# Attention and channel mix on one core: the receptance unit ahead of the tail scores, and two units in three pairs

## The chip, the cores and the metric

The kernel runs on one core of a Trainium2 chip. The metric is the device time of one execution in microseconds. The kernel before took 929.22 us, the median of three executions (929.09 to 930.02). One further execution was recorded by the hardware profiler; every duration below comes from it.

## The reference

Two layers follow each other, all in 32-bit floating point, with 8 sequences of 448 positions.

```python
# attention: 12 heads of 64, no softmax, a sigmoid instead
scores = scale * np.matmul(q, k.transpose(0, 1, 3, 2)) - np.log(S)
attn = 1.0 / (1.0 + np.exp(-scores))
x = np.matmul(attn, v)                    # heads side by side: [8, 448, 768]
# channel mix
xk = mu_k * x + (1.0 - mu_k) * x_prev     # x_prev: x one position earlier
xr = mu_r * x + (1.0 - mu_r) * x_prev
k = np.maximum(xk @ w_k, 0.0)             # 768 -> 1024
v = k * k @ w_v                           # 1024 -> 768
r = 1.0 / (1.0 + np.exp(-(xr @ w_r)))     # receptance, 768 -> 768
return r * v
```

The three weight matrices arrive as 64-bit floats, so the kernel turns their bits into 32-bit numbers itself.

## The kernel before

The two heads that share 128 partitions form a pair; there are 48 pairs, six to a sequence. Every 32-bit matrix product of the scores and of the channel mix is made from three products of a rounded high part and a low remainder (`hi`, `lo`), so each operand is prepared as two tiles: ScalarE rounds, VectorE subtracts (`prepare`, L295 and L296, for the queries and keys).

For pair n the attention loop puts onto TensorE, in this order: three chunks of scores for 128 keys each (`scores`, L322, six matmuls, both heads at once), the weighing of pair n-1 by its values (`weigh`, L351), in every even pair the tails of two pairs' weighing (`weigh_tails`, L360), the scores of the last 64 keys (`score_tail`, L331, three matmuls), and from pair 7 on one unit of the receptance (`receptance`, L386 to L388, 18 matmuls). A unit is one block of 128 output rows for one sequence; 40 units run in pairs 7 to 46, and the rest behind the loop. After two pairs' tails `gather` copies the sums out, mixes each position with its predecessor and splits the result into the units' operands `xr` (L369 to L375), kept for two sequences.

The scores live in three tiles of PSUM, `sc`, each with two halves of 512 columns. `turn(n, c)` picks the tile: chunks 0 to 2 and the tail (c = 3) of the pairs follow each other round the three. A chunk fills both halves, the tail only half 0, and the pair's unit uses half 1 of the tail's tile. ScalarE turns scores into weights (`sigmoid`, L343: `pf` for chunks, `pt` for the tail) and the unit's sums into `ro` (L392), which SyncE's queue stores to `r_d`.

The weights are converted during the loop, mostly on VectorE: first the 12 half rows of w_r (`convert_wr`, L222 to L226, L243 and L244), and then w_k and w_v (`convert_seven`), whose combinations go back to memory and are loaded again near the end of the loop and behind it.

All of this is handed to a small planner, `Plan`. Each operation has an engine, an estimated cost, a priority (mostly the pair number plus a fraction), and the keys that it reads and writes. The planner simulates the engines: whenever one is free, the ready operation of lowest priority starts. The simulated starts give the order in which the instructions are written out, and each engine runs its own in that order. Every TensorE operation of the loop also writes one key, "order", so these stay in the order in which the program names them. The waits on the chip are put in by the tile framework from the order of reads and writes of each tile.

Priorities of the w_r conversions go up by `WR_PACE`, those of the others by `W_PACE` per step. The second half of the kernel, from about 518 us on, is a stretch of matrix products with seven combinations per block (L592).

Of the kernel before, what the change touches and what calls it, by code (L numbers as in the profile page):

```python
# [10 lines left out]
AF = mybir.ActivationFunctionType  # L11
# [11 lines left out]
class Plan:  # L23
# [7 lines left out]
    def op(self, engine, cost, prio, run, reads, writes, dma=None):  # L31
        i = len(self.ops)
        deps = set()
        for r in reads:
            if r in self.writer:
                deps.add(self.writer[r])
        for w in writes:
            if w in self.writer:
                deps.add(self.writer[w])
            deps.update(self.readers.get(w, ()))  # L40
        for r in reads:
            self.readers.setdefault(r, []).append(i)
        for w in writes:
            self.writer[w] = i
            self.readers[w] = []
        deps.discard(i)
        self.ops.append(Op(engine, cost, prio, run, deps, dma))
# [50 lines left out]
def attention_then_channel_mix(  # L98
# [14 lines left out]
    nc = tc.nc  # L113
    P = 128
    N, _, S = q.shape
# [3 lines left out]
    NP = DM // P  # L119
# [4 lines left out]
    NC = S // P  # L124
# [21 lines left out]
    r_d = [[dram.tile([P, S], F32, name=f"r_d{i}_{b}") for b in range(B)] for i in range(NJ)]  # L146
# [3 lines left out]


    WP, PFB, PTB, LEAD = 512, 6, 4, 2
    WR_PACE, W_PACE = 0.45, 0.75
    LATE = 2


    def ring(pool, name, bufs, shape, dtype):
        return [pool.tile(shape, dtype, name=f"{name}{i}") for i in range(bufs)]
# [17 lines left out]
    ro = ring(rpool, "ro", 2, [P, S], F32)  # L176
# [5 lines left out]
    vn = ring(apool, "vn", 5, [P, NV, D], F32)  # L182
# [4 lines left out]
    pf = ring(apool, "pf", PFB, [P, 2, S], F32)  # L187
# [3 lines left out]
    sc = ring(pscore, "sc", 3, [P, 2, 512], F32)  # L191
    av = ring(psum, "av", 2, [P, 512], F32)

    plan = Plan()
    op = plan.op
    SP, PE, ACT, DVE = "SP", "PE", "ACT", "DVE"
    SWITCH = 190

    def mm(n, cols=S):
        return n * (cols * 0.447 + 3)  # L200

    def act(n, sbuf=False, ptr=False):
        return 51 + 0.834 * n + 42 * sbuf + 93 * ptr

    def dve(n, fast=False, ptr=False):
        return 69 + n / (1.92 if fast else 0.96) + 61 * ptr

    def dma(dst, src, prio, reads, writes):
        ns = dst.shape[0] * math.prod(dst.shape[1:]) * 4 / 300
        op(SP, 500, prio, lambda: nc.sync.dma_start(dst, src), reads, writes, dma=ns)  # L210
# [76 lines left out]
    def load(n, at):  # L287
        dma(kn[n % 2], k[n], at, [], [("kn", n % 2)])
        dma(qn[n % 2], q[n], at, [], [("qn", n % 2)])
        dma(vn[n % 5], v[n], at, [], [("vn", n % 5)])  # L290
# [9 lines left out]
    def pe(cost, go, reads, writes, at):  # L300

        op(PE, cost, at, go, reads, writes + ["order"])

    def products(n):
        i = n % LEAD
        return ((kh[i], qh[i]), (kl[i], qh[i]), (kh[i], ql[i]))

    def qk(n):
        i = n % LEAD
        return [(a, i) for a in ("kh", "kl", "qh", "ql")]  # L310


    def turn(n, c):
        return (n * (NC + 1) + c) % 3
# [11 lines left out]
    def score_tail(n, at):  # L326
        u = turn(n, NC)

        def go():
            for e, (kk, qq) in enumerate(products(n)):  # L330
                nc.tensor.matmul(sc[u][:, 0, :S], kk[:, NC * P:], qq, start=e == 0, stop=e == 2)  # L331

        pe(mm(3) + SWITCH, go, qk(n), [("sc", u, 0)], at)

    def sigmoid(n, c, at):
        u = turn(n, c)
        if c < NC:
            i = (n * NC + c) % PFB
            f, s, w, K, R = pf[i], sc[u][:, :, :S], 2 * S, ("pf", i), [("sc", u, 0), ("sc", u, 1)]
        else:  # L340
            i = n % PTB
            f, s, w, K, R = pt[i], sc[u][:, 0, :S], S, ("pt", i), [("sc", u, 0)]
        op(ACT, act(w), at, lambda: nc.scalar.activation(f, s, AF.Sigmoid, bias=NEG_LOG_S, scale=SCALE), R, [K])  # L343


    def weigh(n, c, at):
        i = (n * NC + c) % PFB

        def go():
            for h in range(2):  # L350
                nc.tensor.matmul(av[n % 2][half[h], :S], vn[n % 5][:, h * NC + c, :], pf[i][:, h, :], start=c == 0, stop=False)  # L351

        pe(900 + SWITCH * (c == 0), go, [("pf", i), ("vn", n % 5)], [("av", n % 2)], at)


    def weigh_tails(n, at):
        def go():
            for m in (n, n + 1):
                for r in range(2):
                    nc.tensor.matmul(av[m % 2][half[r ^ (m % 2)], :S], vn[m % 5][half[r], 2 * NC, :], pt[m % PTB][half[r], :], start=False, stop=True)  # L360

        reads = [x for m in (n, n + 1) for x in (("pt", m % PTB), ("vn", m % 5))]
        pe(950, go, reads, [("av", 0), ("av", 1)], at)

    def gather(n, at):
        b, j = divmod(n, NP)
        x, y = xx[n % 2], t1[n % 2]
        X, T = ("xx", n % 2), ("t1", n % 2)
        op(ACT, act(S), at, lambda: nc.scalar.copy(x[:, 1:], av[n % 2][:, :S]), [("av", n % 2)], [X])  # L369
        dma(x_d[j][b], x[:, 1:], at, [X], [("x_d", n)])  # L370
        op(ACT, act(S, True, True), at, lambda: nc.scalar.mul(y, x[:, :S], omr[:, j:j + 1]), [X, ("om", 0)], [T])  # L371
        op(DVE, dve(S, ptr=True), at, lambda: nc.vector.scalar_tensor_tensor(y, x[:, 1:], mur[:, j:j + 1], y, ALU.mult, ALU.add), [X, T], [T])  # L372
        t, key = xr[j][:, :, b % 2 * S:(b % 2 + 1) * S], ("xr", j, b % 2)
        op(ACT, act(S, True), at, lambda: nc.scalar.copy(t[:, 0], y), [T], [key + ("hi",)])
        op(DVE, dve(S), at, lambda: nc.vector.tensor_sub(t[:, 1], y, t[:, 0]), [T, key + ("hi",)], [key + ("lo",)])  # L375

    def receptance(b, i, at, bank):
        t, tk = bank
        u = (b * NJ + i) % 2
        rows = slice(i * P, (i + 1) * P)  # L380
        for j in range(NJ):
            keys = [("xr", j, b % 2, a) for a in ("hi", "lo")]

            def go(j=j):
                hi, lo = (xr[j][:, a, b % 2 * S:(b % 2 + 1) * S] for a in range(2))
                nc.tensor.matmul(t[:, :S], wr_hi[j][:, rows], hi, start=(j == 0), stop=False)  # L386
                nc.tensor.matmul(t[:, :S], wr_lo[j][:, rows], hi, start=False, stop=False)  # L387
                nc.tensor.matmul(t[:, :S], wr_hi[j][:, rows], lo, start=False, stop=(j == NJ - 1))  # L388

            nh = i * P // HN  # L390
            pe(mm(3), go, keys + [("wr", j, nh), (("wr", j, nh), "lo")], [tk], at)
        op(ACT, act(S), at, lambda: nc.scalar.activation(ro[u], t[:, :S], AF.Sigmoid), [tk], [("ro", u)])  # L392
        dma(r_d[i][b], ro[u], at, [("ro", u)], [("r_d", i, b)])

    ORDER = (0, 1, 5, 4, 6, 2, 3)
    POS = {p: g for g, p in enumerate(ORDER)}
# [24 lines left out]
    jt = 0.0  # L421
    for nh in range(2):
        for j in range(NJ):
            convert_wr(j, nh, jt)
            jt += WR_PACE
    jt = max(6, jt)
    for w, out7, half_rows, n in ((w_k, wk_o, NJH, DF // 2), (w_v, wv_o, NFH, HN)):
        for t in range(half_rows):
            convert_seven(w, out7, t, half_rows, n, W_PACE, jt + 0.4)
# [1 line left out]
    units = [(b, i) for b in range(B - 1) for i in range(NJ)]  # L431
    late = units[len(units) - LATE:]
    units = units[:len(units) - LATE]
    for n in range(N + 1):
        if n + 2 < N:
            load(n + 2, n + 0.2)
        if n < N:
            if n + 1 < N:
                prepare(n + 1, n + 0.6)
            for c in range(NC):  # L440
                scores(n, c, n)
                sigmoid(n, c, n + 0.1 * c)
        if n:
            for c in range(NC):
                weigh(n - 1, c, n)
            if n % 2 == 0:
                weigh_tails(n - 2, n)
                gather(n - 2, n + 0.45)
                gather(n - 1, n + 0.5)
        if n < N:  # L450
            score_tail(n, n)
            sigmoid(n, NC, n + 0.5)
        if n > NP and units:
            b, i = units.pop(0)
            u = turn(n, NC)
            receptance(b, i, n + 0.4, (sc[u][:, 1], ("sc", u, 1)))
    late = units + late
    for g in range(2):
        load_weight(0, ORDER[g], N - 6 + 3 * g)
# [87 lines left out]
    op = plan.op  # L547
    units = late + [(B - 1, i) for i in range(NJ)]
    banks = [(sc[i][:, h], ("sc", i, h)) for i in range(3) for h in range(2)]
# [4 lines left out]
        if g < AHEAD:  # L554
            right(0, 0, ORDER[g], 10 * g + 5)
    for u, (b, i) in enumerate(units):
        receptance(b, i, 10 * u, banks[u % 6])
    with tc.manual_schedule():
        plan.emit()
    psc.close()  # L560
# [16 lines left out]
    op = plan.op  # L577
# [67 lines left out]
    for stage in range(2):  # L645
        rows = DF // 2 // P if stage == 0 else HN // P
        for s in range(NS):
            for g, p in enumerate(ORDER):
                at = (stage * NS + s) * 7 + g
# [58 lines left out]
```

## Time and profile before

| | |
|---|---|
| median of three executions | 929.22 us |
| the profiled execution's own time | 932.01 us |
| its span | 930.2 us |
| mean granted TensorE clock | 0.990 |
| TensorE busy | 879.8 us |
| VectorE busy | 572.9 us |
| ScalarE busy | 500.4 us |

The span runs from the first to the last instruction of the execution. Busy time counts an engine's instructions; an engine's idle time before an instruction is put down to whatever released it last. Rows of a timeline give the start, the duration, the engine, the line, the operation with the tile that it writes and the tiles that it reads, and in brackets the idle time before it and who ended it. Rows of merged instructions have a count at the end. Rows of windows give the stretch, its length, the busy time (and instructions) of TensorE, its weight loads, VectorE, ScalarE and GpSimd, the granted clock, the share of the DMA engines and GB/s.

### The profile page before, as it was taken

The numbers are of one execution on the slowest core, as the hardware profiler recorded it, in microseconds if no ns is written. First come the engines' busy times: TensorE is split into PE (matmuls) and PEld (weight loads), VectorE is DVE, ScalarE is ACT, GpSimd is POOL, SyncE is SP. The second block draws the span as 40 slices with busy tenths as digits, with TensorE's granted clock in tenths as the row PEclk, the third lists the DMA queues.
The fourth block names the chain that finished last, engine by engine and source line by source line (L and its number), as shares of the span: only waits on it lengthen the run. The fifth ranks groups of instructions, "written<-read, shape, count | busy, mean of one in ns | idle before, by whom it ended". The sixth has DMA issues, their size and how long they took to land.

```text
span 930.2 us, 13102 instructions
## 1 busy us (share of the span) xinstructions
PE 879.8 (95%) x4656; PEld 684.6 (74%) x4656; DVE 572.9 (62%) x1039; ACT 500.4 (54%) x858; POOL 0.5 (0%) x8
## 2 busy tenths in 40 slices
PE   6889999999999999999989999999999999999998
PEld 3446566656665666566558899999999999999997
DVE  5999877852222232222225789696968978695955
ACT  5785666655565666556555756556464533233330
POOL 0000000000000000000000000000000000000000
PEclk8899999999999999999999999999999999999999
DMA  7679997863333434334127556334365556465514
GB/s 257 205 252 335 302 318 241 280 215 102 122 115 103 135 111 132 102 106 130 50 92 245 175 174 197 119 139 129 125 228 161 199 163 216 132 196 178 159 60 148
DMA packets 90929, 159.21 MB, mean 171 GB/s; under 512 B 10352, under 2 KB 73328, under 8 KB 90864
## 3 DMA queue, kind: packets, MB, share of 16 engines
q1 hardware_dynamic: 90864, 158.38, 52.6%
q8 instruction: 36, 0.59, 0.3%
q14 instruction: 29, 0.24, 0.1%
HBM read 99.62 MB, written 58.72 MB: 170 GB/s over the span
## 4 chain that ended last, share of the span: by engine, by line
PE 91%; ACT 4%; DVE 2%; issue 2%; DMA 1%; SPq 0%; POOLq 0%; POOL 0%; ACTq 0%; DVEq 0%
PE xb L592 25%; PE yb L592 19%; PE av L351 12%; PE sc L322 10%; PE sc L386 7%; PE sc L388 6%; PE sc L387 6%; PE sc L331 4%; ACT pt L343 2%; PE av L360 2%; DMA wraw<-in_moe_w_r 1%; DVE wbits L226 0%; SPq L210 0%; ACT t L371 0%; ACT pf L343 0%
## 5 line engine op out<-in xcount | busy, mean ns | idle before, releaser
L386 PE MATMUL sc<-xr,slot 128*128 128x448 f32 x288 | 110.7, 384 | 30.9 <-ACT pt L343 25.3
L517 ACT CAST rr<-ys 128x448 fp32r<-128x448 f32 x135 | 73.9, 567 | 105.0 <-PE yb L592 40.6
L343 ACT ACTIVATE pf<-sc 128x896 f32<-128x896 f32 x144 | 122.7, 920 | 12.7 <-PE sc L322 12.7
L351 PE MATMUL av<-pf,vn 128*64 128x448 f32 x576 | 121.4, 557 | 0.0
L372 DVE SCALAR_TENSOR_TENSOR t<-xx,mur,t 128x448 f32<-128x448 f32 x48 | 30.7, 681 | 136.7 <-ACT t L371 136.7
L387 PE MATMUL sc<-xr,slot 128*128 128x448 f32 x288 | 105.9, 368 | 0.0
L388 PE MATMUL sc<-xr,slot 128*128 128x448 f32 x288 | 105.8, 367 | 0.0
L592 PE MATMUL xb<-rr,slotb 128*128 128x448 f32 x450 | 93.4, 365 | 0.7 <-issue 0.7
L592 PE MATMUL yb<-rr,slot 128*128 128x448 f32 x450 | 93.9, 364 | 0.0
L296 DVE TENSOR_TENSOR kl<-kn,kh 128x512 fp32r<-128x512 f32 x48 | 33.1, 690 | 97.2 <-ACT kh L295 97.2
L386 PEld LDWEIGHTS sc<-xr,slot 128*128 128x128 f32 x288 | 54.4, 189 | 51.8 <-ACT pt L343 40.2
L518 DVE TENSOR_TENSOR rr<-ys,rr 128x448 fp32r<-128x448 f32 x135 | 80.4, 618 | 19.5 <-ACT rr L517 19.4
L592 PEld LDWEIGHTS xb<-rr,slotb 128*128 128x128 f32 x450 | 84.4, 188 | 7.7 <-issue 1.1
L592 PEld LDWEIGHTS yb<-rr,slot 128*128 128x128 f32 x450 | 84.4, 187 | 6.7
L351 PEld LDWEIGHTS av<-pf,vn 128*64 128x64 f32 x576 | 37.8, 139 | 61.5 <-issue 60.4
L322 PE MATMUL sc<-qh,kh 64*128 64x448 f32 x288 | 59.6, 410 | 7.5 <-ACT qh L295 6.6
L392 ACT ACTIVATE ro<-sc 128x448 f32<-128x448 f32 x48 | 26.2, 545 | 67.4 <-PE sc L388 59.9
L322 PE MATMUL sc<-ql,kh 64*128 64x448 f32 x288 | 55.1, 379 | 6.0 <-DVE ql L296 6.0
L343 ACT ACTIVATE pt<-sc 128x448 f32<-128x448 f32 x48 | 26.1, 545 | 60.7 <-PE sc L388 55.7
L388 PEld LDWEIGHTS sc<-xr,slot 128*128 128x128 f32 x288 | 54.5, 189 | 4.6
L387 PEld LDWEIGHTS sc<-xr,slot 128*128 128x128 f32 x288 | 54.6, 190 | 3.6
L322 PE MATMUL sc<-qh,kl 64*128 64x448 f32 x288 | 54.1, 372 | 1.1 <-DVE kl L296 1.1
(88 smaller groups left out, 1410.0 us busy)
## 6 DMA issues: line engine op xcount, KB each, us to landing
k_d<-cc SPq DMA_DIRECT2D x64, 224.0 KB, 2.0
kn<-in_k SPq DMA_DIRECT2D x48, 256.0 KB, 2.7
qn<-in_q SPq DMA_DIRECT2D x48, 224.0 KB, 3.2
vn<-in_v SPq DMA_DIRECT2D x48, 224.0 KB, 3.1
x_d<-xx SPq DMA_DIRECT2D x48, 224.0 KB, 3.2
r_d<-ro SPq DMA_DIRECT2D x48, 224.0 KB, 2.6
x<-x_d SPq DMA_DIRECT2D x48, 224.0 KB, 2.6
rt<-r_d SPq DMA_DIRECT2D x48, 224.0 KB, 2.9
```

What stands on the lines that cost most here:

```text
L296: op(DVE, dve(w), at, lambda src=src, hi=hi, lo=lo: nc.vector.tensor_sub(lo[i], src[n % 2], hi[i]), [(a + "n", n % 2), (a + "h", i)], [(a ...
L322: nc.tensor.matmul(sc[u][:, h, :S], kk[half[h], c * P:(c + 1) * P], qq[half[h], :], start=e == 0, stop=e == 2)
L331: nc.tensor.matmul(sc[u][:, 0, :S], kk[:, NC * P:], qq, start=e == 0, stop=e == 2)
L343: op(ACT, act(w), at, lambda: nc.scalar.activation(f, s, AF.Sigmoid, bias=NEG_LOG_S, scale=SCALE), R, [K])
L351: nc.tensor.matmul(av[n % 2][half[h], :S], vn[n % 5][:, h * NC + c, :], pf[i][:, h, :], start=c == 0, stop=False)
L372: op(DVE, dve(S, ptr=True), at, lambda: nc.vector.scalar_tensor_tensor(y, x[:, 1:], mur[:, j:j + 1], y, ALU.mult, ALU.add), [X, T], [T])
L386: nc.tensor.matmul(t[:, :S], wr_hi[j][:, rows], hi, start=(j == 0), stop=False)
L387: nc.tensor.matmul(t[:, :S], wr_lo[j][:, rows], hi, start=False, stop=False)
L388: nc.tensor.matmul(t[:, :S], wr_hi[j][:, rows], lo, start=False, stop=(j == NJ - 1))
L517: op(ACT, act(S, True), at, lambda: nc.scalar.copy(r[:, 0], y), [Y], [R])
L518: op(DVE, dve(S), at, lambda: nc.vector.tensor_sub(r[:, 1], y, r[:, 0]), [Y, R], [R + ("lo",)])
L592: nc.tensor.matmul(bank[:, :S], a, b, start=first and t == 0 and e == 0, stop=t == n - 1 and e == 2, skip_group_check=True)
```

## The change

In a pair with a unit, the unit's matmuls are now named before the tail's scores. Its sigmoid `ro` and its store are taken out of the function and called after the tail; `ro` also reads a new key, "tail", that the tail's scores write. Units start at pair 10 instead of 7: pairs 10 to 12 have two each, the first in half 1 of the tile of the next pair's first chunk, and pairs 13 to 46 one each, as before. The conversions of w_r get priorities 0.85 apart (0.45 before), those of w_k and w_v begin at 10.2 instead of 6 and stand 0.9 apart (0.75 before). Four cost estimates of the planner change: a weighing and the tails' weighing cost 752 (900 and 950 before), and the extra 190 for a change of the matmuls' shape goes from the tail's scores to a unit's first step.

```diff
-    WR_PACE, W_PACE = 0.45, 0.75
+    WR_PACE, W_PACE = 0.85, 0.9
+    R_FROM = 10
...
-        pe(mm(3) + SWITCH, go, qk(n), [("sc", u, 0)], at)
+        pe(mm(3), go, qk(n), [("sc", u, 0), "tail"], at)
...
-        pe(900 + SWITCH * (c == 0), go, [("pf", i), ("vn", n % 5)], [("av", n % 2)], at)
+        pe(752 + SWITCH * (c == 0), go, [("pf", i), ("vn", n % 5)], [("av", n % 2)], at)
...
-        pe(950, go, reads, [("av", 0), ("av", 1)], at)
+        pe(752, go, reads, [("av", 0), ("av", 1)], at)
...
-            pe(mm(3), go, keys + [("wr", j, nh), (("wr", j, nh), "lo")], [tk], at)
-        op(ACT, act(S), at, lambda: nc.scalar.activation(ro[u], t[:, :S], AF.Sigmoid), [tk], [("ro", u)])
-        dma(r_d[i][b], ro[u], at, [("ro", u)], [("r_d", i, b)])
+            pe(mm(3) + SWITCH * (j == 0), go, keys + [("wr", j, nh), (("wr", j, nh), "lo")], [tk], at)
+
+        def out():
+            op(ACT, act(S), at, lambda: nc.scalar.activation(ro[u], t[:, :S], AF.Sigmoid), [tk, "tail"], [("ro", u)])
+            dma(r_d[i][b], ro[u], at, [("ro", u)], [("r_d", i, b)])
+
+        return out
...
-    jt = max(6, jt)
+    jt = max(R_FROM, jt)
...
+        done = []
+        for e in range(0 if n < R_FROM else 2 if n < R_FROM + 3 else 1):
+            if units:
+                u = turn(n, NC + 1 - e) if n < R_FROM + 3 else turn(n, NC)
+                done.append(receptance(*units.pop(0), n + 0.4, (sc[u][:, 1], ("sc", u, 1))))
         if n < N:
             score_tail(n, n)
+        for f in done:
+            f()
+        if n < N:
             sigmoid(n, NC, n + 0.5)
-        if n > NP and units:
-            b, i = units.pop(0)
-            u = turn(n, NC)
-            receptance(b, i, n + 0.4, (sc[u][:, 1], ("sc", u, 1)))
...
-        receptance(b, i, 10 * u, banks[u % 6])
+        receptance(b, i, 10 * u, banks[u % 6])()
```

## The prediction

> **What bounds the kernel now.** I read the page's totals first, then TensorE's own waits, then the timeline around one of those waits, and last the first 60 us.
>
> ```profile
> span 930.2 us, 13102 instructions
> PE 879.8 (95%) x4656; PEld 684.6 (74%) x4656; DVE 572.9 (62%) x1039; ACT 500.4 (54%) x858; POOL 0.5 (0%) x8
> ```
>
> TensorE is busy for 95% of the span. What is left is in its list of waits (total us, times, longest us):
>
> ```profile
> PE sc L386 <- ACT pt L343: 25.3, 40, 0.6
> PE sc L322 <- ACT qh L295: 6.6, 4, 4.6
> PE sc L322 <- DVE ql L296: 6.0, 4, 3.5
> ```
>
> The first row is one wait per receptance unit, 40 times: the unit's matmuls (L386) wait until ScalarE has read the last keys' scores (pt, L343). The next two fall at the start. The timeline of an odd pair shows what one wait costs (start us, duration, engine, line):
>
> ```profile
> 311.43 0.47 PE L331 MATMUL sc<-qh,kh 128*128 128x448 f32 x1
> 312.55 0.36 PE L388 MATMUL sc<-xr,slot 128*128 128x448 f32 x1
> 312.94 0.54 ACT L343 ACTIVATE pt<-sc 128x448 f32<-128x448 f32 x1 [2.49 <-PE sc L388]
> 313.38 0.61 ACT L295 CAST kh<-kn 128x512 fp32r<-128x512 f32 x1
> 313.54 0.47 PE L386 MATMUL sc<-xr,slot 128*128 128x448 f32 x1 [0.63 <-ACT pt L343]
> 313.85 0.36 PE L387 MATMUL sc<-xr,slot 128*128 128x448 f32 x1
> 316.48 0.37 PE L388 MATMUL sc<-xr,slot 128*128 128x448 f32 x1
> 316.78 0.47 PE L322 MATMUL sc<-qh,kh 64*128 64x448 f32 x2
> ```
>
> From the L387 at 313.85 to the last L388 at 316.48 are 13 matmuls, so they start 0.202 us apart. Without the wait the L387 would start two steps after 312.55, at 312.95; it starts at 313.85. One wait costs 0.90 us, more than its 0.63 us of idle time, since the row's idle time begins only where the modelled end of the last matmul lies, and the first matmul after it takes 0.31 instead of 0.20 to its successor. Forty waits: 36 us. The wait is between two halves of one tile: pt reads `sc[u][:, 0]`, the unit writes `sc[u][:, 1]`.
>
> **The moved unit.** In the plan every TensorE operation writes the key "order", so TensorE's sequence is the program's sequence; costs can't change it. A unit now runs ahead of the tail scores. Its tile was last read by the pair's first sigmoid, before three weighings, so it finds the tile free. The tail scores follow it on the same engine. ScalarE then reads both halves, ro and pt, after the tail. Removed: the wait. Its place could be taken by the next writer of that tile, the third score chunk of the next pair, which must now wait for two ScalarE reads instead of one. Their chain, from the start of the last matmul: ro starts 0.39 later (312.55 to 312.94), pt 0.44 after ro (312.94 to 313.38), takes 0.54, and TensorE starts 0.06 after its end (313.48 to 313.54): 1.43 us. TensorE's side, by these rows of a pair's start:
>
> ```profile
> 307.00 0.47 PE L322 MATMUL sc<-qh,kh 64*128 64x448 f32 x2
> 307.91 2.54 ACT L343 ACTIVATE pf<-sc 128x896 f32<-128x896 f32 x3 [0.26 <-PE sc L322]
> 308.32 0.36 PE L322 MATMUL sc<-qh,kh 64*128 64x448 f32 x2
> ```
>
> The third chunk comes 1.32 us after the first, which comes 0.30 after the tail's last matmul (316.48 to 316.78): 1.62 us. So 0.19 us to spare, if ScalarE is free for ro. Its load in an even pair, the heavier one:
>
> ```profile
> 301.64 0.47 PE L331 MATMUL sc<-qh,kh 128*128 128x448 f32 x1
> 301.79 0.97 ACT L369 COPY xx<-av 128x448 f32<-128x448 f32 x2 [2.04 <-issue]
> 302.64 1.24 ACT L371 ACTIVATE t<-xx,omr 128x448 f32<-128x448 f32 x2
> 304.82 0.56 ACT L374 CAST xr<-t 128x448 fp32r<-128x448 f32 x1
> ```
>
> If the unit starts where this tail did, at 301.64, then 21 matmuls later the tail's last one starts at 301.64 + 0.31 + 19 x 0.202 = 305.8, and ro is due at 306.2. The gather's copies, multiplications and two casts (0.97 + 1.24 + 2 x 0.56 = 3.3 us from 301.79) end near 305.1, so ScalarE is free. The casts for the pair after next (L295) need the operands that the tail still reads; they come after pt now, with a whole pair until they are used. I take the new wait as zero. Bounds: none, or ScalarE late by one cast (0.56), which is 0.56 - 0.19 + 0.11 = 0.48 us a pair. A gain beyond the 0.90 has no source.
>
> Of pairs with a unit, 10 to 46 are left. For 13 to 46 nothing else changes: **34 x 0.90 = 30.6 us**, bounds 30.6 and 34 x 0.42 = 14.3.
>
> **Two units in pairs 10 to 12.** The first of the two uses the tile of the next pair's first chunk, last read by this pair's second sigmoid, long done. That next chunk then waits for its ro; nothing on the chip makes this ro wait for the tail, and the second unit (18 x 0.202 = 3.6 us) covers it. If ScalarE reaches it only after the tail, it costs up to 0.90, three times. I take 0. Its two r_d stores per pair go on SP's queue; r_d is read only after the attention loop. By pair 11 both halves of w_r are needed; see the next part.
>
> **The start.** Here units move from pairs 7 to 9 into 10 to 12, and the w_r conversions get later priorities (0.85 a pair instead of 0.45; the other weights from 10.2 on, 0.9). The work up to pair 13 is the same, so I compare when that pair starts.
>
> ```profile
> 22.29 0.47 PE L322 MATMUL sc<-qh,kh 64*128 64x448 f32 x2
> 60.45 0.47 PE L322 MATMUL sc<-qh,kh 64*128 64x448 f32 x2
> 100.08 0.47 PE L386 MATMUL sc<-xr,slot 128*128 128x448 f32 x1 [0.63 <-ACT pt L343]
> 120.56 0.47 PE L386 MATMUL sc<-xr,slot 128*128 128x448 f32 x1 [0.63 <-ACT pt L343]
> 122.59 0.47 PE L322 MATMUL sc<-qh,kh 64*128 64x448 f32 x2
> 132.37 0.47 PE L322 MATMUL sc<-qh,kh 64*128 64x448 f32 x2
> ```
>
> Pair 13 starts at 122.59 now and takes 9.78 us; two pairs take 20.48 (100.08 to 120.56), so an even one takes 10.70. Less the wait: 8.88 and 9.80. Less the unit's 3.64: 5.24 and 6.16 without a unit. Pairs 2 to 6 (22.29 to 60.45) took 38.2 us where 3 x 6.16 + 2 x 5.24 = 29.0 would do: 1.8 us a pair lost, to waits for prepared operands and to a lower clock. First, the very start:
>
> ```profile
> 9.89 0.36 DVE L222 TENSOR_SCALAR wbits<-wraw 128x384 uint32<-128x384 uint32 x1 [1.64 <-DMA wraw<-in_moe_w_r]
> 14.38 0.62 DVE L296 TENSOR_TENSOR ql<-qn,qh 128x448 fp32r<-128x448 f32 x1
> 10.27 0.56 ACT L295 CAST qh<-qn 128x448 fp32r<-128x448 f32 x1
> 15.05 0.74 PE L322 MATMUL sc<-ql,kh 64*128 64x448 f32 x2 [3.50 <-DVE ql L296]
> 15.00:22.00 7.00, 6.95 (x29) 3.68 (x29) 6.05 (x14) 3.26 (x5) 0.00 (x0) 0.62 0.75 230
> 36.00:46.00 10.00, 8.15 (x37) 3.73 (x37) 9.42 (x23) 5.60 (x10) 0.00 (x0) 0.66 0.76 237
> ```
>
> ql of pair 1 has its input at 10.83, but VectorE's queue holds two conversions ahead of it (9.89 to 14.38; priorities 0 and 0.45 against 0.6). The second now has 0.85 and comes behind: one conversion, half of 4.5 us, goes from the 3.50 us wait, some 2.3. The windows' granted clock (third number from the end) was 0.62 after that wait; it withheld 38% of 7 us, 2.6 us of work. I take 1.7 of it as regained, for the wait shrinks by two thirds but isn't gone; bounds 0 and 2.6. So pair 2 starts at about 22.3 - 4.0 = 18.3.
>
> By the Trainium skill (TensorE: Matmul & The Clock Gate, section on what is actually happening) the clock halves only after an idle window of about 3.4 us. The window 15 to 22 agrees; that of 36 to 46 does not: its clock was 0.66 with a wait of 1.00 us in it, shown next. By the rule all 2.6 us would come back and the sum would be 0.9 lower; by the second window perhaps nothing would.
>
> ```profile
> 38.33 0.74 PE L322 MATMUL sc<-ql,kh 64*128 64x448 f32 x2 [1.00 <-DVE ql L296]
> 61.79 0.53 ACT L343 ACTIVATE pt<-sc 128x448 f32<-128x448 f32 x1
> 62.37 0.47 PE L322 MATMUL sc<-qh,kh 64*128 64x448 f32 x2 [0.44 <-ACT pt L343]
> 46.00:60.00 14.00, 12.39 (x80) 6.19 (x77) 12.65 (x26) 11.83 (x21) 0.00 (x0) 1.00 0.68 227
> 60.00:66.29 6.29, 5.85 (x37) 3.13 (x35) 6.15 (x12) 6.26 (x12) 0.00 (x0) 1.00 0.84 260
> ```
>
> Pairs 2 to 9, eight now, have no unit. VectorE's conversions no longer stand ahead of pairs' operands, but ScalarE is nearly full there: 11.83 us of busy time for two pairs (46 to 60), 6.26 of 6.29 in the last row, so about 5.9 to 6.3 a pair against TensorE's mean 5.70; and in even pairs pt stands behind the gather (61.79), which costs some 0.7. Removing VectorE's delay thus uncovers ScalarE. I take a loss of 0.9 us a pair: between the floor of 0.2 (5.9 less 5.70) and 1.8 as now. Pair 10 starts at 18.3 + 4 x (6.16 + 5.24) + 8 x 0.9 = 71.1. Pairs 10 to 12 with two units each: 13.44 + 12.52 + 13.44 = 39.4. Pair 13 starts at 110.5 instead of 122.59: **12.1 us**. Bounds: 17.4 + 45.6 + 1.6 + 39.4 = 104.0 (18.6 gained), and 22.3 + 45.6 + 14.4 + 39.4 = 121.7 (0.9 gained). A loss has no source: per pair neither ScalarE nor VectorE gets more to do than in pairs 2 to 6 now.
>
> **What costs nothing.** The later pace of the conversions: they end by about 205 now, and most weights are wanted only at pair 42 or later.
>
> ```profile
> 55.85 0.55 DVE L244 TENSOR_TENSOR slot<-wbits,slot 128x384 fp32r<-128x384 f32 x1
> 175.00:200.00 25.00, 23.73 (x140) 14.38 (x137) 18.56 (x40) 14.71 (x25) 0.00 (x0) 1.00 0.81 263
> 200.00:225.00 25.00, 23.10 (x129) 15.63 (x127) 7.60 (x13) 16.16 (x28) 0.00 (x0) 1.00 0.43 135
> ```
>
> VectorE's busy time falls from 18.56 to 7.60 of 25 us there, so a delay of tens of us is covered by hundreds. If w_r were late for pair 10, the cover would be gone and TensorE would stand still at once; but the last of its 12 conversions runs at 55.85 now, and they are wanted from about 75 on. The planner's costs (752 for a weighing, the switch moved to the unit) can only reorder ScalarE, VectorE and SP; that is inside the bounds of 0 to 0.48 us a pair above.
>
> **The sum.** The profiled execution took 932.0 us (span 930.2 and 1.8 around it), 2.8 above the median of 929.2. 932.0 - 30.6 - 12.1 = 889.3; as a median, 929.2 - 42.7 = 886.5, say **887**.
>
> **Rivals.**
> The wait comes back in part at the third chunk of the next pair: 0.19 us is little, and ro and pt are late by a cast wherever the order sends one ahead of them; against it, ScalarE's idle 2.49 us ahead of pt at 312.94. Price up to 37 x 0.48 = 18 us: about 896 to 904. 0.13.
> The start gains nothing: ScalarE, 6.26 of 6.29 us, holds eight pairs at 1.8 us of loss. 929.2 - 30.6 - 0.9 = 898. 0.15.
> The change doesn't do what it says: the tail waits for ro's read of the other half, as the unit does for pt today. For it: the same tile tracking; against: ro is put behind the tail by the key "tail". Then only the start gains: 917. 0.04.
> Slower: ScalarE takes the next pair's first sigmoid ahead of ro and pt. It can start 1.21 us after the tail's last matmul (0.30, and 307.00 to 307.91) and takes 0.85 (2.54 for three); ro and pt take 0.44 + 0.54 behind it, so the third chunk starts near 3.1 instead of 1.62 and the following units move with it: 1.48 and the 0.11 of a fresh start, 1.6 us in 37 pairs, 59 us against 42.7 gained: about 945. It decides from 42.7 / 37 = 1.15 us a pair. Against it: pt's priority is n + 0.5, that sigmoid's n + 1. 0.03.
>
> **Chances.** 0.65 for the forecast, whose own range is 881 to 893. What a measurement here tells from no change is about 0.2%, 2 us. Faster holds all cases but the slower one and a sliver near zero: 0.96, 0.01, 0.03. The range takes in the weak start and most of the returned wait: 881 to 900.
>
> **What would show it.** The wait of L386 for pt gone from TensorE's list and no new row of L322 for pt or ro above 5 us in pairs 13 to 46: two pairs take 18.7 us. Pair 13 starts near 110. Wrong: a two-pair period above 19.2, a start of pair 13 after 117, or a wait of L386 for converted w_r.

## The result, and the profile after

The changed kernel took **891.34 us**, the median of four executions (890.72 to 893.66), against 929.62 for the kernel before (929.09 to 931.51) in the same comparison: a ratio of 0.959, with a 95% interval of 0.957 to 0.961. That is 38.3 us less; 42.7 were predicted. The two profiled executions are 932.01 and 891.54, so 40.5 apart: the one of before was 2.4 us above its median.

The page's totals of the changed kernel, and then TensorE's waits (total us, times, longest us):

```profile
span 889.8 us, 13099 instructions
PE 866.3 (97%) x4656; PEld 685.5 (77%) x4656; DVE 574.8 (65%) x1039; ACT 494.3 (56%) x858; POOL 0.5 (0%) x8
```

```profile
PE sc L323 <- ACT qh L296: 8.2, 6, 4.6
PE sc L387 <- ACT ro L395: 5.7, 4, 3.6
PE sc L323 <- ACT pt L344: 1.8, 4, 0.5
PE sc L323 <- DVE kl L297: 1.4, 2, 1.0
PE sc L323 <- DVE ql L297: 1.3, 2, 1.1
```

The row of 25.3 us, the unit's wait for pt, is gone. The unit's matmuls (now L387 to L389) wait only for ro, behind the loop, as before. The four waits of the third chunk for pt, 1.8 us, stand in pairs 3, 5, 7 and 9, which have no unit; the kernel before had two like them, 0.9 us. In pairs with a unit none has come in the old wait's place. The timeline of one pair's end and the next one's start shows why:

```profile
289.00 0.37 PE L389 MATMUL sc<-xr,slot 128*128 128x448 f32 x1
289.21 0.37 PE L332 MATMUL sc<-qh,kh 128*128 128x448 f32 x1
...
289.61 0.36 PE L332 MATMUL sc<-ql,kh 128*128 128x448 f32 x1
289.90 0.47 PE L323 MATMUL sc<-qh,kh 64*128 64x448 f32 x2
290.01 0.54 ACT L395 ACTIVATE ro<-sc 128x448 f32<-128x448 f32 x1 [4.50 <-PE sc L332]
...
290.45 0.54 ACT L344 ACTIVATE pt<-sc 128x448 f32<-128x448 f32 x1
...
291.23 0.37 PE L323 MATMUL sc<-qh,kh 64*128 64x448 f32 x2
```

The tail (L332) follows the unit in one step of 0.21 us. ro starts 0.40 us after the tail's last matmul, pt 0.44 after ro and ends at 290.99, and the third chunk starts at 291.23. With the 0.06 us that TensorE takes to start after a read, 0.18 us were to spare.

Where the 40.4 us of the span came from can be read off the starts of a few pairs. Pairs 2, 10, 13 and 47 of the changed kernel, and pair 47 of before below them:

```profile
18.32 0.47 PE L323 MATMUL sc<-qh,kh 64*128 64x448 f32 x2
72.38 0.47 PE L323 MATMUL sc<-qh,kh 64*128 64x448 f32 x2 [0.28 <-ACT qh L296]
112.64 0.47 PE L323 MATMUL sc<-qh,kh 64*128 64x448 f32 x2
430.40 0.47 PE L323 MATMUL sc<-qh,kh 64*128 64x448 f32 x2
```

```profile
470.84 0.47 PE L322 MATMUL sc<-qh,kh 64*128 64x448 f32 x2
```

| stretch | before | after | gain | predicted |
|---|---|---|---|---|
| to pair 13 | 122.59 | 112.64 | 9.95 | 12.1 |
| pairs 13 to 46 | 348.25 | 317.76 | 30.49 | 30.6 |
| from pair 47 to the end of the span | 459.4 | 459.4 | 0.0 | 0 |

### The profile page after: what moved, and what is told of

Same layout as the page of the kernel before. It is cut to its first block, busy times and chain, and to the rows that moved or that the text cites. A ratio compares the mean times of both kernels' runs of the same rounds, so it can differ in the third digit from the quotient of the medians.

```text
span 889.8 us, 13099 instructions
## 1 busy us (share of the span) xinstructions
PE 866.3 (97%) x4656; PEld 685.5 (77%) x4656; DVE 574.8 (65%) x1039; ACT 494.3 (56%) x858; POOL 0.5 (0%) x8
## 4 chain that ended last, share of the span: by engine, by line
PE 92%; DMA 3%; DVE 2%; issue 1%; ACT 1%; SPq 0%; ACTq 0%; DVEq 0%; POOLq 0%
PE xb L601 26%; PE yb L601 20%; PE av L352 12%; PE sc L323 10%; PE sc L387 7%; PE sc L389 6%; PE sc L388 6%; PE sc L332 3%; PE av L361 2%; DMA x_d<-xx 1%; DMA qn<-in_q 1%; DMA wraw<-in_moe_w_r 1%; DVE ql L297 0%; ACT t L372 0%; DMA x<-x_d 0%
## 5 line engine op out<-in xcount | busy, mean ns | idle before, releaser
L352 PE MATMUL av<-pf,vn 128*64 128x448 f32 x576 | 118.8, 548 | 0.0
L387 PE MATMUL sc<-xr,slot 128*128 128x448 f32 x288 | 110.4, 383 | 5.7 <-ACT ro L395 5.7
L389 PE MATMUL sc<-xr,slot 128*128 128x448 f32 x288 | 106.0, 368 | 0.0
L395 ACT ACTIVATE ro<-sc 128x448 f32<-128x448 f32 x48 | 26.2, 546 | 117.5 <-PE sc L332 94.3
L387 PEld LDWEIGHTS sc<-xr,slot 128*128 128x128 f32 x288 | 54.5, 189 | 37.8 <-issue 14.1
L389 PEld LDWEIGHTS sc<-xr,slot 128*128 128x128 f32 x288 | 54.5, 189 | 4.6
L323 PEld LDWEIGHTS sc<-qh,kh 64*128 64x128 f32 x288 | 27.7, 188 | 27.9 <-issue 11.5
```

Of the source, the lines that this page charges most:

```text
L323: nc.tensor.matmul(sc[u][:, h, :S], kk[half[h], c * P:(c + 1) * P], qq[half[h], :], start=e == 0, stop=e == 2)
```

## The experiments

For each kernel, the start of pairs 2 and 13 and the length of pairs 13 to 46 come from the same rows of its profiled execution; the time is its median. The kernel before measured 929.6 to 930.6 beside them.

| kernel | pair 2 starts | pair 13 starts | pairs 13 to 46 | median |
|---|---|---|---|---|
| before | 22.29 | 122.59 | 348.25 | 929.6 |
| changed | 18.32 | 112.64 | 317.76 | 891.3 |
| order_only | 20.50 | 114.78 | 320.85 | 898.5 |
| order_costs | 21.41 | 119.17 | 320.49 | 898.9 |
| start_only | 19.99 | 115.51 | 348.16 | 924.4 |
| read_late | 18.44 | 116.72 | 317.79 | 894.7 |
| extra1 | 17.82 | 117.89 | 332.20 | 911.6 |
| extra3 | 18.30 | 120.78 | 362.42 | 946.5 |
| gather_late | 19.41 | 115.55 | 320.39 | 895.5 |
| copy_dve | 19.77 | 112.63 | 317.91 | 889.8 |
| late_wk | 18.02 | 186.15 | 317.42 | 966.6 |
| copy_late | 16.82 | 185.43 | 317.41 | 964.7 |
| paces_only | 16.64 | 108.13 | 317.64 | 887.4 |
| units_only | 20.83 | 123.44 | 317.55 | 901.4 |

The theory had two terms: the wait (30.6) and the start (12.1). The rivals were that the wait comes back at the third chunk, that the start gains nothing, and that the order of the two writes does not matter or does not help.

### The order alone, and the start alone

order_only is the changed kernel with the paces, the units and the planner's costs of before:

```diff
-    WR_PACE, W_PACE = 0.85, 0.9
+    WR_PACE, W_PACE = 0.45, 0.75
-        for e in range(0 if n < R_FROM else 2 if n < R_FROM + 3 else 1):
+        for e in range(1 if n > NP else 0):
-                u = turn(n, NC + 1 - e) if n < R_FROM + 3 else turn(n, NC)
+                u = turn(n, NC)
```

and with 6 for `R_FROM` as the first start of the other conversions, and 900, 950 and the two `SWITCH` places as before.

> Only the order: the unit ahead of the tail's scores, ro behind the tail; units from pair 7, one a pair, with the paces and planner's costs of before. Theory (the 40 waits of the unit for pt are gone, 0.90 us each, and the start stays as it was): 929.6 - 36 = about 893.6, pair 7 still starts near 60.5, two pairs take 18.7 us. Rival (the order's gain depends on the new costs, which place ro and pt): the third score chunk waits for pt, 0.5 us a pair or more, above 910.

It took 898.49 us, a ratio of 0.966 (0.964 to 0.968): 31.4 us less than before, where 36 were expected. No wait for pt is left in the pairs with units, but pairs 13 to 46 took 320.85 us and not 317.8. No wait explains the difference; the unit's matmuls ran at another rate, as these rows show, which is worth some 2.7 us of the 4.6 that are missing. The remaining 1.9 us are less than starts vary: order_only and order_costs (below) have the same paces and units and start pair 13 at 114.78 and 119.17.

```profile
291.83 0.37 PE L387 MATMUL sc<-xr,slot 128*128 128x448 f32 x1
...
293.07 0.37 PE L332 MATMUL sc<-qh,kh 128*128 128x448 f32 x1
```

Six steps in 1.24 us are 0.2067 each (0.2063 in the mean of a unit), against 0.2025 in most pairs of the changed kernel; with 21 such matmuls in a pair that is 0.08 us a pair, 2.7 us in 34 pairs.

start_only is the kernel before with the new paces and with two units in pairs 10 to 12, behind the tail:

```diff
+    R_FROM = 10
-        if n > NP and units:
-            b, i = units.pop(0)
-            u = turn(n, NC)
-            receptance(b, i, n + 0.4, (sc[u][:, 1], ("sc", u, 1)))
+        for e in range(0 if n < R_FROM else 2 if n < R_FROM + 3 else 1):
+            if units:
+                b, i = units.pop(0)
+                u = turn(n, NC + 1 - e) if n < R_FROM + 3 else turn(n, NC)
+                receptance(b, i, n + 0.4, (sc[u][:, 1], ("sc", u, 1)))
```

> Only the start: two units in pairs 10 to 12, the new paces, units behind the tail as before, planner's costs of before. Theory: pair 2 starts near 18.3, pair 13 near 112 to 113, for the first of two units covers the read of pt; then 34 waits of 0.90 us stay. 929.6 - 10 = about 919.6. Rival (the start's gain needs the new order or costs): 925 or more.

It took 924.39 us, 0.993 (0.992 to 0.995) of before, 5.5 us less and not 10. Pairs 13 to 46 are as before, and the wait is there once in each (TensorE's waits of this kernel):

```profile
PE sc L387 <- ACT pt L344: 21.5, 34, 0.6
```

Thirty-four times, as expected: where two units stand in a pair, the first covers the read. The start gained less, since pair 2 came at 19.99 and pairs 2 to 9 were slower too.

### Is it the order of the writes, or the read between them?

read_late puts the tail ahead of the unit again, but both of ScalarE's reads behind the unit:

```diff
+        if n < N:
+            score_tail(n, n)
         for e in range(0 if n < R_FROM else 2 if n < R_FROM + 3 else 1):
...
-        if n < N:
-            score_tail(n, n)
...
-            f, s, w, K, R = pt[i], sc[u][:, 0, :S], S, ("pt", i), [("sc", u, 0)]
+            f, s, w, K, R = pt[i], sc[u][:, 0, :S], S, ("pt", i), [("sc", u, 0), ("sc", u, 1)]
```

> The changed kernel with the tail's scores ahead of the unit, as before, but both reads of ScalarE (ro and pt) behind the unit. Theory (what costs is a ScalarE read between two TensorE writes of one tile, whichever write is first): as the changed kernel, 891 within 1.5 us, and no wait of the unit. Rival (the unit has to be ahead of the tail): the 37 waits come back, about 921 to 924.

Pairs 13 to 46 took 317.79 us, as in the changed kernel, with no wait of the unit for pt: the read between two writes of one tile was the cost, and the order of the writes does not matter. TensorE's waits of this kernel:

```profile
PE sc L323 <- ACT qh L296: 8.6, 6, 4.6
PE sc L387 <- ACT ro L395: 6.1, 4, 3.5
PE sc L323 <- DVE kl L297: 2.7, 1, 2.7
PE sc L323 <- ACT pt L344: 1.7, 4, 0.4
```

The whole took 894.68 and so missed the expected time by 3.4; pair 13 started at 116.72, 4.1 us later. In the start pair 8 took 11.0 us there, and no pair without a unit took above 7.9 in the changed kernel. Its wait for kl was the 2.7 us of the list, 1.05 in the changed kernel, and behind it the granted clock was 0.50 from 64 to 67 us, where the changed kernel had 1.00.

The Trainium skill (PSUM — Partial Sum Buffer, Summary: rules for kernel authors) asks for a guard between an engine's read and a matmul by bank, and half of this tile is one bank by its figures. So the chip may not need the wait that stood here, and it would come only from the tile being tracked as a whole. That is not shown: no run here split the tile to try it.

### How much room the third chunk has

extra1 adds one ScalarE read of the tail's scores into a scrap tile ahead of ro; extra3 has three in place of the one:

```diff
+        if done and n < N:
+            for e in range(1):
+                again(n, n + 0.3 + 0.01 * e)
         for f in done:
             f()
...
+    def again(n, at):
+        u = turn(n, NC)
+        op(ACT, act(S), at, lambda: nc.scalar.activation(junk, sc[u][:, 0, :S], AF.Sigmoid), [("sc", u, 0), "tail"], ["junk"])
```

> The changed kernel with one more ScalarE read of the tail's scores into a scrap tile ahead of ro, in each pair with a unit. Theory (0.19 us to spare at the third chunk): the chain of three reads is 1.43 + 0.44 = 1.87 us against 1.62, so the third chunk waits 0.25 and loses 0.36 a pair, 37 pairs: 13 us, about 904. Rival (there is more room than that, ScalarE's reads are off the path): 891 to 892. Second rival (no room at all, and ro already late): 0.55 a pair, 911.

> The changed kernel with three more ScalarE reads of the tail's scores ahead of ro. Theory (each read behind the room of 0.19 us costs its 0.44): the pair is longer than with one extra read by 0.88, so about 1.33 above the changed kernel's, 37 x 1.33 = 49, and pairs 10 to 12 a little more: about 940 to 944, slower than the kernel before. Rival (reads overlap with matmuls in some other way): below 930.

extra1 took 911.6 us. That is the second rival's time, but not by its way: a pair from 13 to 46 is (332.20 - 317.76) / 34 = 0.42 longer and not 0.55, with 0.08 of it from the matmuls' slower rate, seen here too; 0.36 were expected. Pair 13 starts 5.3 us later than in the changed kernel. Of this, 3.1 us lie in pairs 10 to 12, where the scrap read waits for the tail and so holds up the first unit's ro behind it, about 1 us a time, and 2.7 in pairs 2 to 9, where pair 8 is long as in read_late (10.6 us); pair 2 came 0.5 earlier. With 14.4 us in pairs 13 to 46 that is the 20 us by which it is slower; 13 were expected. One pair of extra1:

```profile
302.56 0.37 PE L333 MATMUL sc<-ql,kh 128*128 128x448 f32 x1
302.86 0.47 PE L324 MATMUL sc<-qh,kh 64*128 64x448 f32 x2
...
303.98 0.37 PE L324 MATMUL sc<-ql,kh 64*128 64x448 f32 x2
304.50 0.47 PE L324 MATMUL sc<-qh,kh 64*128 64x448 f32 x2
```

The third chunk starts 1.64 us after the first, and not 1.33 (289.90 to 291.23). These 34 waits have no row in TensorE's list: the last matmul before starts at 303.98 and ends by the model 0.37 later, which leaves 0.15 us of idle time. extra3 has a row:

```profile
PE sc L324 <- ACT junk L350: 33.7, 34, 1.0
```

It took 946.5 us, slower than before (ratio 1.017), 1.31 a pair above the changed kernel where 1.33 was expected, again with 0.08 from the slower rate. Against extra1, whose rate is the same, its two further reads cost (362.42 - 332.20) / 34 = 0.89 us a pair. So each read behind the room costs its 0.44 us, and the whole change would be a loss from 38.3 / 37 = 1.04 us a pair.

### What bounds the start

gather_late lets ScalarE read pt ahead of the gather's multiplications, copy_dve moves the gather's copies to VectorE:

```diff
-                gather(n - 2, n + 0.45)
-                gather(n - 1, n + 0.5)
+                gather(n - 2, n + 0.52)
+                gather(n - 1, n + 0.55)
```

```diff
-        op(ACT, act(S), at, lambda: nc.scalar.copy(x[:, 1:], av[n % 2][:, :S]), [("av", n % 2)], [X])
+        op(DVE, dve(S), at, lambda: nc.vector.tensor_copy(x[:, 1:], av[n % 2][:, :S]), [("av", n % 2)], [X])
```

> The changed kernel with the gather's priorities 0.52 and 0.55 instead of 0.45 and 0.5, so that in pairs without a unit ScalarE reads the tail's scores (pt) after the gather's first copy and not after its multiplications. Theory (in pairs 2, 4, 6 and 8 the third chunk of the next pair waits for a pt that stands behind the gather, 0.6 and 0.1 each): 4 x 0.7 = 2.9 us less, about 888.5. Rival (ScalarE is full there, so what is put off is missed later, as waits for qh and kl): 891.3 within 1 us.

> The changed kernel with the gather's two copies out of PSUM on VectorE instead of ScalarE. Theory (ScalarE bounds pairs 2 to 9): ScalarE gets 0.43 us a pair less to do there, pair 10 starts up to 3.4 us earlier than 72.4, about 888. Rival (VectorE bounds them: 24.3 and 23.0 of 25 us busy in the second and third 25 us): it gets 0.6 us a pair more, pair 10 starts up to 4.8 us later, 893 to 896. From pair 13 on no difference by either.

gather_late took 895.5 us (a ratio of 0.960 to 0.963), not faster than the changed kernel; 2.6 us of the difference lie in pairs 13 to 46, by the slower rate of the matmuls. Its waits for pt are gone, and the waits for qh grew from 8.2 to 12.6 us. What was put off was missed later. copy_dve took 889.8 (887.9 to 892.8, a ratio of 0.957 with 0.954 to 0.959), which is not told apart from the changed kernel's 0.959. Its pairs 2 to 9 took 52.8 us instead of 54.1; the waits for pt went, those for qh grew to 12.0.

late_wk holds the conversions of w_k and w_v back until the tail of pair 9: `others` is the loop over `convert_seven`, moved there, and `hold` is empty for w_r and holds the key "tail" for the rest. copy_late does this and copy_dve's edit:

```diff
+        if n == R_FROM:
+            others(jt)
...
-        dma(raw[:, :n, :].rearrange("p n t -> p (n t)"), src, at - 1.5, [], [R])
+        dma(raw[:, :n, :].rearrange("p n t -> p (n t)"), src, at - 1.5, hold, [R])
```

> The changed kernel with the loads of w_k and w_v put behind the tail of pair 9 in the plan, so that no conversion of these two stands between the operands of pairs 6 to 9. ScalarE's work stays. Theory (both engines are nearly full in pairs 2 to 9, so relieving one gives little): only the two waits for kl, 1.4 us, go: pair 10 starts near 71, 890. Rival (VectorE alone bounds): pairs 6 to 9 come down to 5.70 each, pair 10 starts near 68, 887.

> The run copy_dve (the gather's copies on VectorE) and late_wk together: both engines are relieved. Theory (both bound together): pairs 2 to 9 take 50 to 51 us instead of 54.1, below either change alone (copy_dve took 52.8), 886 to 887. Rival (what limits is the order within the queues, not the load): as copy_dve, about 890.

Both are slower than the kernel before as whole kernels, at 966.6 and 964.7 us. My edit made every load read the key that the tail of pair 10 writes, so that tail was planned behind all of them, and ScalarE's queue got casts of reloaded weights ahead of ro. One of them held ScalarE, and through it TensorE, for more than 40 us (late_wk):

```profile
123.70 0.83 ACT L416 CAST slotb<-wop 128x768 fp32r<-128x768 f32 x1 [42.77 <-DMA wop<-wk_o]
...
133.16 0.97 ACT L395 ACTIVATE ro<-sc 128x448 f32<-128x448 f32 x2
```

What comes behind pair 10 says nothing on the question, but pairs 2 to 9 lie ahead of it. Pair 10 started at 71.60 in late_wk (72.38 in the changed kernel), so pairs 2 to 9 took 53.6 us instead of 54.1. A granted clock of 0.89 from 25 to 40 us, where the changed kernel had 1.00, hides up to 1.7 us of the gain: pairs 6 to 9, which the held conversions had stood in, took 25.7 instead of 27.4, near the 1.4 us that were expected. In copy_late pairs 2 to 9 took 54.1 us (16.82 to 70.96), where 50 to 51 were expected if load were the limit; the clock was 0.89 in the same window. Its last 13 us ahead of pair 10, which are pairs 8 and 9 (stretch, length, busy TensorE, weight loads, VectorE, ScalarE, GpSimd, then clock, DMA share, GB/s), and the same stretch of copy_dve:

```profile
58.00:71.00 13.00, 11.66 (x76) 5.87 (x76) 7.55 (x15) 10.64 (x19) 0.00 (x0) 1.00 0.68 228
```

```profile
58.00:71.00 13.00, 11.58 (x75) 5.99 (x74) 13.00 (x27) 10.65 (x20) 0.00 (x0) 1.00 0.80 265
```

VectorE's 13.00 fell to 7.55, ScalarE had 2.4 us free, and TensorE did no more. So load is not what holds pairs 8 and 9 at 13.1 us in both kernels. The rival that names the order within the queues is left there, though no run changed that order alone to show it. For the pairs ahead of them the runs do not decide: VectorE stayed nearly full in copy_late too, 14.11 of 15 us from 25 to 40 and 14.92 from 40 to 55.

### Which part of the start gains

paces_only keeps order, costs and paces of the changed kernel and has one unit a pair from pair 7 on; units_only keeps its units and has the paces of before; order_costs has both as before, so that it is order_only with the new costs. The first two changes below are those of paces_only and order_costs, the last two those of units_only and order_costs:

```diff
-        for e in range(0 if n < R_FROM else 2 if n < R_FROM + 3 else 1):
+        for e in range(1 if n > NP else 0):
-                u = turn(n, NC + 1 - e) if n < R_FROM + 3 else turn(n, NC)
+                u = turn(n, NC)
-    WR_PACE, W_PACE = 0.85, 0.9
+    WR_PACE, W_PACE = 0.45, 0.75
-    jt = max(R_FROM, jt)
+    jt = max(6, jt)
```

> Only the order, as in the run of that name, but with the changed kernel's four planner costs. TensorE's order is the same. Theory (the costs do nothing; the units' matmuls of order_only, 0.206 us apart instead of 0.2025, belong to that execution or program): pairs 13 to 46 take 318 to 321 us and the whole 893 to 898.5. Rival (the costs are what keeps ScalarE's reads ahead): pairs 13 to 46 take 318 us with the new costs only, the whole is 893 to 894.5, and the start doesn't move.

> The changed kernel with one unit in each pair from 7 on, as before; order, paces and planner's costs are the new ones. Theory (the paces make the start's gain, and pairs 7 to 9 lose their 1.06 us each only because they have no unit to hide ScalarE's work): pair 13 starts 3 us earlier than 112.6, near 109.5, 888. Rival (the units' later start is needed, w_r or the operands come too late for pair 7): 891 or more, with waits of the unit's first matmul for w_r.

> The changed kernel with the paces of before (0.45 from 0, then 0.75 from 6); order, units and planner's costs are the new ones. Theory (the paces make the start's gain): pair 2 starts at 20 to 22, pairs 2 to 6 lose 1.8 us each again, pair 13 starts near 116 to 119, 895 to 898. Rival (the paces do nothing, since the planner never lets a free engine stand while a conversion is ready): 891 to 892.

| | paces of before | new paces |
|---|---|---|
| one unit from pair 7 | 898.90 (order_costs) | **887.37** (paces_only) |
| two units in pairs 10 to 12 | 901.36 (units_only) | 891.34 (changed) |

By these medians the new paces gain 11.5 us with the units as before and 10.0 with the new ones, and the units' later start costs 2.5 and 4.0. The first number of each is blurred: of the four kernels only order_costs has the matmuls' slower rate, which makes its pairs 13 to 46 some 2.8 us longer. Less that, the paces gain about 8.7 there and the units cost about 5.3. Of the 4.0 us, 1.7 stand already at the start of pair 2 (18.32 and 16.64), ahead of any unit, where both kernels have run the same instructions in the same order. From pair 2 to pair 13 the changed kernel takes 2.8 us more than paces_only (94.3 and 91.5). The costs do nothing that shows: order_costs and order_only are 0.4 us apart, and the matmuls' slower rate is in both. **paces_only beats both kernels**: a ratio of 0.953 (0.952 to 0.955), 886.6 to 888.0 against 890.7 to 893.7.

How the paces gain is in pairs 1 to 6. Pair 7 starts at 61.96 in order_costs and at 51.06 in paces_only, 10.9 us earlier, in the profiled executions (that of order_costs is 3.0 us above its median). order_costs waits as before, its VectorE holding two conversions ahead of ql, and paces_only does not wait there. TensorE's waits for ql in order_costs, and four windows of order_costs and then of paces_only:

```profile
15.27 0.74 PE L323 MATMUL sc<-ql,kh 64*128 64x448 f32 x2 [3.88 <-DVE ql L297]
53.61 0.74 PE L323 MATMUL sc<-ql,kh 64*128 64x448 f32 x2 [2.47 <-DVE ql L297]
```

```profile
10.00:25.00 15.00, 10.41 (x61) 5.98 (x63) 12.99 (x31) 9.40 (x16) 0.00 (x0) 0.77 0.79 240
25.00:40.00 15.00, 13.13 (x76) 6.78 (x74) 14.71 (x33) 13.37 (x24) 0.00 (x0) 0.89 0.69 218
40.00:55.00 15.00, 10.66 (x64) 5.31 (x62) 13.60 (x31) 10.59 (x21) 0.00 (x0) 0.91 0.68 219
55.00:70.00 15.00, 14.60 (x77) 7.71 (x74) 12.74 (x24) 9.08 (x15) 0.00 (x0) 0.86 0.82 252
```

```profile
10.00:25.00 15.00, 13.46 (x88) 6.94 (x88) 12.39 (x30) 12.22 (x22) 0.00 (x0) 1.00 0.81 261
25.00:40.00 15.00, 11.90 (x74) 5.70 (x74) 14.66 (x33) 12.55 (x23) 0.00 (x0) 1.00 0.74 217
40.00:55.00 15.00, 14.18 (x88) 6.90 (x90) 13.27 (x30) 14.01 (x26) 0.00 (x0) 1.00 0.86 252
55.00:70.00 15.00, 15.00 (x86) 10.38 (x83) 14.21 (x27) 10.02 (x18) 0.00 (x0) 1.00 0.77 238
```

The granted clock stands at 1.00 throughout in paces_only and at 0.77, 0.89, 0.91 and 0.86 in order_costs. The clock withheld there is 15 x (0.23 + 0.11 + 0.09 + 0.14) = 8.6 us. Counted by windows of 1 us, and only as far as TensorE was busy in them, it is about 6.1. By this estimate a little over half of the 10.9 is clock; the shorter waits are the rest. The paces do not set the clock by themselves: from 10 to 25 us the changed kernel had 0.89 and copy_dve 0.77 with the new paces, and order_only had 1.00 with the old ones.

## Why the prediction was right, and where its terms were off

**The moved unit: right.** 0.90 us a wait, 34 waits, 30.6 predicted and 30.49 measured; two pairs take 18.67 us where 18.7 were named. The room of 0.19 was 0.18 in the trace, and extra1 and extra3 show that reads behind it cost what its step says. read_late narrows the reason: not that the unit comes first, but that nothing reads between the writes.

**The start: right in sign, mis-sized.** 12.1 predicted, 9.95 measured between the profiled executions. As that of before was 2.4 us above its median, the medians put it nearer 38.3 - 30.5 = 7.8. The term "a loss of 0.9 us a pair" for pairs 2 to 9 measured (72.38 - 18.32 - 45.6) / 8 = 1.06, 1.3 us in all, and pairs 10 to 12 took 40.3 instead of 39.4. Pair 2 came at 18.32 where 18.3 was named, and the wait for ql went from 3.50 to 1.08 us, 2.4 where 2.3 was taken; but this start varies among the profiled executions, from 16.64 to 19.99 with the new paces, so the agreement is partly luck.

**The cause named for that loss did not hold where it was tried.** The prediction said that removing VectorE's delay uncovers a full ScalarE. In pairs 8 and 9 of copy_late ScalarE is busy for 10.64 of 13 us and VectorE for 7.55, and the pairs are no shorter than in copy_dve. The waits move between pt, qh and kl from kernel to kernel. Which wait comes is shown; what sets the floor of some 6.4 to 6.6 us a pair there is open, and so is what bounds pairs 2 to 7.

**"A loss has no source" was wrong for a part.** The units' later start is a loss by itself, 4.0 us by the medians and 2.8 of it between pairs 2 and 13, hidden under the paces' gain. The prediction had its mechanism, eight pairs without a unit instead of five, but added it into one term and so did not see that a part of the change was worth undoing.

**The clock.** The prediction took back 1.7 of 2.6 us at pair 2 and nothing later. The runs put more weight on it. In windows of 1 us the granted clock is 1.00 or 0.50, but for those in which it changes, and each fall withholds 1.7 us or twice that. From 8 to 62 us this adds up to 6.8 us before, 1.7 in the changed kernel, 8.6 in order_costs and 0 in paces_only. It differs between executions of one kernel too: the profiled one of before had a mean clock of 0.990 and took 932.01 us, while those with 0.994 took 929.2 to 930.6.

By the Trainium skill (TensorE: Matmul & The Clock Gate, section on what is actually happening) an idle window of about 3.4 us halves it. The halves agree; the length does not show in a single wait. The 3.88 us wait of order_costs began at 11.39, shortly behind one of 1.61, and the clock fell between 11 and 12 already; it fell again between 52 and 53, inside the wait of 2.47 us, which came shortly behind one of 1.62:

```profile
11.00:12.00 1.00, 0.39 (x4) 0.01 (x2) 0.96 (x4) 0.00 (x0) 0.00 (x0) 0.72 1.06 404
12.00:13.00 1.00, 0.00 (x0) 0.00 (x0) 1.00 (x4) 0.44 (x2) 0.00 (x0) 0.50 1.13 334
52.00:53.00 1.00, 0.00 (x0) 0.00 (x0) 1.00 (x4) 0.00 (x0) 0.00 (x0) 0.70 0.81 295
```

In the kernel before, whose window from 15 to 22 the prediction took to agree, the clock fell between 13 and 14, some 2 us into the wait of 3.50. paces_only kept a clock of 1.00 through a wait of 2.44 us with no other close ahead of it:

```profile
31.43 0.47 PE L323 MATMUL sc<-qh,kh 64*128 64x448 f32 x2 [2.44 <-ACT qh L296]
```

**The rivals.** The wait at the third chunk did not come back in pairs with a unit. The start gained. The tail does not wait for ro. The slower case, which was to decide from 1.15 us a pair, did not come; extra3 made its price by other means, 1.31 us a pair, and was slower than before by 1.7%.

## What to carry to other kernels

Here a read between two writes of one tile made the second write wait, even though the two touch different halves; put both writes first and both reads behind, and reckon the room by the next writer of that tile. A wait of an engine costs what the distance between its instructions' starts shows, here 0.90 us, and not the idle time of its row, 0.63. Where a change has several parts with one aim, time them apart: here one of them, the later units, cost some 3 to 4 us of what the others gained.

## What was not expected of the hardware

The unit's matmuls start either 0.2025 or 0.2063 us apart, with the clock granted at 1.00 in both cases. In order_only all units from pair 13 on are at 0.206, and in gather_late all from pair 15 on; in the changed kernel pairs 10, 12, 14 and 17 to 19 are, and from pair 20 to 46 none. It is worth 2.7 us over pairs 13 to 46, more than half of what order_only took beyond its expectation and part of what gather_late did. What sets it stays open; the order of TensorE's instructions does not explain it, since order_only and paces_only run the same TensorE order and only order_only is slow from pair 18 on. No wait of TensorE is listed in these pairs of either.
